# Group 1 joins the block products: its second product with wo3 in seven half-size products, and the sums for wo3 made in group 0's stage 7

## The chip, the core and the metric

One NeuronCore of one Trainium2 chip runs the whole program. The metric is device time in microseconds (us), the median of the runs; lower is better. The engines are TensorE (PE in the profile, its weight loads PEld), VectorE (DVE), ScalarE (ACT), GpSimd (POOL) and SyncE (SP), which issues every DMA of this kernel. Engines take their instructions in order and wait for each other through semaphores.

## The reference

Eight batches of attention through 32 packed rows, then two feed-forward layers over 4608 tokens of width 512, in fp32:

```python
p_packed = sm_attn(p, k, v)              # per head, softmax(p k^T / 8) v
x = sm_attn(q, p_packed, p_packed)       # tokens x 512
x = (silu(x @ w_gate) * (x @ w_val)) @ w_out         # d_ff 1536
a, b = x @ w1, x @ w2                                # d_ff 1024
return (a * b @ w3) @ w_out2                         # w3 1024 x 1024, w_out2 1024 x 512
```

## The kernel before

The change lies in the last layer. `w3 @ w_out2` is multiplied out once, as wo3 (1024 x 512), in pieces between the work of the layer ahead of it; what remains is `(x w1 * x w2) @ wo3`. Every fp32 operand is split into a high and a low part (`split`: a cast on ScalarE, a subtraction on VectorE or GpSimd, line 89 in the profile), and each product is three matmuls: high by high, high by low, low by high.

The tokens go in six groups of 768 (`g`, two halves of TH = 384). A group has two stages.

**Stage 5** (`stage5`, matmuls on line 1111) computes ab = (x w1) * (x w2) for eight blocks `f` of 128 features. Both products over two token halves are done as seven block products (`PROD`: sums and differences of weight blocks, S1 to S4, by sums and differences of x, T1 to T4) instead of eight. The sums accumulate in PSUM banks A, B and C: ScalarE copies bank A after product 0 (`keep("s1", A)`), and product 2 adds to the same bank, so product 2 cannot start before that copy. The weight blocks ws (f, k) are made in group 0 (`ws_sums`, `ws_block`) and stored to DRAM (wsd). From then on they are read back: one by one for group 1 (`ws_load`, line 833), in pairs for groups 2 to 5 (`ws_pair`, line 1018).

**Stage 7** multiplies ab by wo3. Groups 0 and 1 do it plainly (`stage7`, line 1201): per 128 tokens, 8 blocks f by three matmuls of 512 columns, with wo3_hi and wo3_lo held in SBUF. Groups 2 to 5 do it in seven block products (`stage7s`, line 1225): sums of ab (`pair_tasks`) by blocks and sums of wo3, 256 columns wide, whose split halves are loaded from DRAM (wobd, `wob_load`). `GS = 2` is the number of plain groups.

The wobd blocks are made during stage 5 of group 1 (`wob_task`): for each i of four, two rows of wo3 are loaded (wo3e), four differences T1 to T4 formed (line 1051, tile wo3s), seven blocks split (wobs) and stored (line 1059). A table `wob_at` says in which block f and behind which product k each step is issued.

Inputs of the next group, x2, are loaded, subtracted and split by `x2_prep` (lines 838, 843, 89): for the plain groups in four parts just ahead of stage 7.

SBUF is held in pools. `mp` has wo3_hi, wo3_lo and what the plain groups need, `wst` fourteen weight blocks of 256 columns. When the last plain group is done both are released and `mp2` takes their bytes: tile wsx for every fifth pair, kA to kD for the copies out of PSUM, the sums of ab, two blocks wob. All pools are made with `reuse_waits="tile"`: a tile waits for every user of an earlier tile on its bytes. wsx, kC, kB, ab0 and kA, the first tiles of mp2, lie on the bytes of wo3_hi.

This last part stands in `with tc.manual_schedule(...)`: each engine issues in the order in which the program is written. The layer ahead of it (lines 897 to 986) is put in order by a scheduler instead. There, `pin` and `behind` give it hints: while `pin` holds an instruction under a name, an instruction issued through `behind` with that name is kept behind it. `w3_task` converts, transposes and multiplies the rows of w3 and w_out2 in pieces: `w3_conv` converts (through `conv`, whose instructions ask for the pins "act" and "dve"), and `w3_step` transposes and multiplies. `w3_at[1]` and `w3_at[2]` are the last accumulation and the last activation of the first unit of the last batch pair.

Of the kernel before, what the change touches and what calls it, by code (L numbers as in the profile page):

```python
# [8 lines left out]
F32 = mybir.dt.float32  # L9
F32R = mybir.dt.float32r  # L10
# [3 lines left out]
ALU = mybir.AluOpType  # L14
# [24 lines left out]
def packed_attention_moe_kernel(  # L39
# [768 lines left out]
    def ws_tile(g, f, k):  # L808
        if f == 0:
            if k % 2 == 0:  # L810
                wg_at.append(wgv.tile([128, 2, 2, 256], F32R, tag=("wh", "wl")[k // 2 % 2], name=f"ws0_{k}"))
            t = wg_at[-1][:, k % 2]
        else:
            t = wst.tile([128, 2, 256], F32R, tag="wst", name=f"ws{g}_{f}_{k}", bufs=14)
        ws_t[f, k] = t
        return t
# [8 lines left out]
    def ws_at(f, k):  # L825
        i, half = divmod(7 * f + k, 2)
        return wsd[i][:, half]
# [1 line left out]
    def ws_store(f, k):  # L829
        nc.sync.dma_start(ws_at(f, k), ws_t[f, k].bitcast(F32))  # L830

    def ws_load(g, f, k):
        nc.sync.dma_start(ws_tile(g, f, k).bitcast(F32), ws_at(f, k))

    def x2_load(g, i, j):
        t = xp.tile([128, 2, TH], F32, tag="x2r", name=f"x2r{g}_{i}{j}", bufs=3)
        c0 = 2 * TH * g + TH * j
# [40 lines left out]
    def w3_task(P, f, slot):  # L878

        if P < NPR - 1 or slot not in W3S[f % GF] or f > 9 or (f == 0 and slot < 3):  # L880
            return
        i = w3_at[0]
        w3_at[0] += 1
        if 0 < i <= len(w3_list) and w3_list[i - 1].startswith("w3"):
            if NH <= i < 2 * NH:
                pin.update(dve=w3_at[1], act=w3_at[2])
            new = tuple(int(x) for x in w3_list[i - 1].split("_")[1:])
            pin.clear()
            w3_step(new, w3_old[0])
            w3_old[0] = new  # L890
            if new[1] == NF2 - 1:
                w3_step(None, new)
                w3_old[0] = None
        if i < len(w3_list):
            w3_conv(w3_list[i])

    for n, (P, f) in enumerate(steps):
        def at(i):
# [107 lines left out]
    def split_wo3(r):  # L1006
        split(wo3_hi[:, r], wo3_lo[:, r], wo3_t.pop(r))

    GS = 2
    NPB = NF2 // 2  # L1010
    pair_t, wob_t, abT, later = {}, {}, {}, []

# [22 lines left out]

    wo3_b = {}

    def wob_task(i, n):

        if n == 0:  # L1040
            e, o = (vl.tile([128, DM], F32, tag=("vt", "vu")[i % 2], name=f"wo3e{i}_{r}") for r in range(2))
            for r, t in enumerate((e, o)):
                nc.sync.dma_start(t, wo3d[1, 2 * i + r])
            b = wo3_b[i] = {"B11": e[:, 0:256], "B12": e[:, 256:512], "B21": o[:, 0:256], "B22": o[:, 256:512]}
            return
        b = wo3_b[i]
        if n == 1:
            t = xp.tile([128, 4, 256], F32, tag="wf", name=f"wo3s{i}")
            for at, (name, x, y) in enumerate((("T1", "B12", "B11"), ("T2", "B22", "T1"),
                                               ("T3", "B22", "B12"), ("T4", "B21", "T2"))):  # L1050
                nc.vector.tensor_tensor(out=t[:, at], in0=b[x], in1=b[y], op=ALU.subtract)
                b[name] = t[:, at]
            return
        k = n - 2
        if (7 * i + k) % 2 == 0:
            wo3_b["to"] = wgv.tile([128, 2, 2, 256], F32R, tag=("wh", "wl")[(7 * i + k) // 2 % 2], name=f"wobs{i}_{k}")
        t = wo3_b["to"][:, (7 * i + k) % 2]
        split(t[:, 0], t[:, 1], b[PROD[k][2]], sub_on="pool" if k % 2 else "dve")
        nc.sync.dma_start(wobd[k][:, i], t.bitcast(F32))

    wob_at = {}
    for i in range(NPB):
        wob_at[((0, 4), (1, 0), (2, 4), (4, 4))[i]] = [(i, 0)]
        for n in range(1, 7):
            wob_at[2 * i + 1, n] = [(i, n)]
        if i + 1 < NPB:
            wob_at[2 * i + 2, 1], wob_at[2 * i + 2, 2] = [(i, 7)], [(i, 8)]

    def block(i, name, src, on):
        hl = tuple(mp2.tile([128, TH], F32R, tag=f"{name}{x}{i}", name=f"{name}{x}{i}") for x in "hl")  # L1070
# [27 lines left out]
    def stage5(g, f):  # L1098
# [16 lines left out]
        def ahead(k):  # L1115

            if g == 0 and f + 1 < NF2:
                ws_block(f + 1, k)
            n = (NF2 - 1) * g + f + 1
            ng, nf = divmod(n, NF2 - 1)  # L1120
            if f and 0 < ng < GS:
                ws_load(ng, nf + 1, k)
            if g == GS - 1 and f == 0:
                ws_store(0, k)
            i = 56 * (g - GS) + 7 * f + k
            if g >= GS and i % 2:
                pair_t.pop(i // 2)
                ws_pair(i // 2 + 5)
            if g == GS - 1:
                for x in wob_at.pop((f, k), ()):  # L1130
                    wob_task(*x)
            if g >= GS and 0 < k < 6 and later:
                later.pop(0)()

# [56 lines left out]
    def stage7(g):  # L1191
        for tb in range(2 * TH // 128):
            j, cols = tb // 3, slice(128 * (tb % 3), 128 * (tb % 3) + 128)
            t = bank(f"po{g}_{tb}")
            for f in range(NF2):
                abh, abl = ab_t[f]
                for a, w, first, last in (
                    (abh, wo3_hi, f == 0, False), (abh, wo3_lo, False, False),
                    (abl, wo3_hi, False, f == NF2 - 1),
                ):  # L1200
                    nc.tensor.matmul(t, lhsT=a[:, j, cols], rhs=w[:, f], start=first, stop=last)  # L1201
            o = vl.tile([128, DM], F32, tag="vu", name=f"o{g}_{tb}")
            nc.scalar.copy(o, t)
            r0 = 2 * TH * g + 128 * tb
            nc.sync.dma_start(out[r0:r0 + 128, :], o)

    def stage7s(g):
        bkA, bkB = ([bank(f"po{n}{g}_{m}")[:, 0:256] for m in range(3)] for n in "AB")
# [39 lines left out]
    with tc.manual_schedule(engines=M0):  # L1248
        for g in range(NG2):
            for f in range(NF2):  # L1250
                stage5(g, f)
                if g == 0:
                    if f + 2 < NF2:
                        ws_sums(f + 2)
                    if f + 3 < NF2:
                        load_w12(f + 3)
                    split_wo3(f)
                    if f + 1 < NF2:
                        load_wo3(f + 1)
                if g == GS and f in (2, 4, 6):  # L1260
                    wob_load(f // 2 - 1)
            if g < GS:
                ab_split.pop()()
                if g == GS - 1:
                    wob_task(NPB - 1, 7)
                    wob_task(NPB - 1, 8)
                for part in range(4):
                    x2_prep(g + 1, part)
                if g == GS - 1:
                    for n in range(4):  # L1270
                        ws_pair(n)
                stage7(g)
            else:
                if g + 1 < NG2:
                    x2_prep(g + 1, 0)
                while later:
                    later.pop(0)()
                stage7s(g)
            if g == GS - 1:
                assert not wob_at  # L1280
                mp.release()
                wst.release()
                mp2 = pool("mp2", "right")
                ws_pair(4)
# [38 lines left out]
```

## Time and profile before

| | |
|---|---|
| median of 3 runs | 1352.88 us (1351.63 to 1355.17) |
| the profiled execution | 1352.85 us, span 1351.0 us |
| TensorE busy | 1327.5 us, 98% |
| VectorE, ScalarE, GpSimd busy | 734.5, 607.9, 466.1 us |
| group 0, stage 5 and stage 7 | 806.9 to 867.9 to 901.3 us |
| group 1 | 901.3 to 961.2 to 993.9 us |
| group 2 | 993.9 to 1052.4 to 1082.9 us |

The span is the time from the first to the last instruction that the profiler saw; the time of the execution is 1.85 us more. Stage bounds are the starts of the first matmul of each stage. Busy shares are of the span.

### The profile page before, as it was taken

To read this page: it belongs to the slowest core of one execution; us is meant where nothing else is said; L and a number is where in the kernel's file an instruction comes from. 1 tells how busy PE (TensorE), PEld (TensorE's weight loads), DVE (VectorE), ACT (ScalarE), POOL (GpSimd) and SP (SyncE) were. 2 spreads that over 40 slices of the span, in tenths; PEclk is the share of its full clock that TensorE was granted. 3 is DMA by queue.
4 is the path that set the end of the run, shared out by engine and by line. 5 is a ranking of instruction groups with operands and counts; after the bars stand their busy time and mean duration, and the time that the engine had idled before them with its cause. 6 is when DMAs were issued, how large, how long until landed. Compare 5 with 4: busy or idle time off the path is not lost.

```text
span 1351.0 us, 26605 instructions
## 1 busy us (share of the span) xinstructions
PE 1327.5 (98%) x10628; PEld 1251.9 (93%) x10628; DVE 734.5 (54%) x1114; ACT 607.9 (45%) x1068; POOL 466.1 (35%) x385
## 2 busy tenths in 40 slices
PE   8989999999999999999999999999999999999999
PEld 6679899999999999989999999889899999999999
DVE  4766877336564466562363379636535535456352
ACT  5774644244443444344554246435334334345241
POOL 1332322323322333243444226404315245153261
PEclk9999999999999999999999999999999999999999
DMA  9987766524455444234443149949769898978865
GB/s 308 344 241 214 216 194 194 167 74 130 148 128 180 121 127 126 71 124 139 145 148 111 55 164 322 342 138 334 256 234 307 315 308 267 327 252 280 311 205 172
DMA packets 192348, 278.32 MB, mean 206 GB/s; under 512 B 71008, under 2 KB 124256, under 8 KB 189920
## 3 DMA queue, kind: packets, MB, share of 16 engines
q1 hardware_dynamic: 192224, 276.62, 63.6%
q8 instruction: 84, 1.38, 0.4%
q14 instruction: 40, 0.33, 0.1%
HBM read 217.84 MB, written 58.72 MB: 205 GB/s over the span
## 4 chain that ended last, share of the span: by engine, by line
PE 76%; DVE 6%; DMA 4%; issue 1%; ACT 1%; SPq 0%; POOL 0%; DVEq 0%; ACTq 0%; POOLq 0%
PE px L675 19%; PE pA L1111 11%; PE pg L446 10%; PE pv L446 9%; PE pB L1111 6%; PE po L1201 4%; PE poA L1225 4%; PE pw L767 3%; PE poB L1225 3%; PE pC L1111 3%; PE pc L413 2%; DMA x2r<-X2d 1%; DMA wo3r<-wo3d 1%; DVE ws L89 1%; DMA ws<-wsd 1%
## 5 line engine op out<-in xcount | busy, mean ns | idle before, releaser
L89 POOL TENSOR_TENSOR ul<-u,uh 128x576 fp32r<-128x576 f32 x96 | 145.5, 1517 | 304.7 <-ACT uh L96 278.6
L675 PE MATMUL px<-uh,woh 128*128 128x384 f32 x576 | 148.1, 338 | 0.2
L455 DVE TENSOR_TENSOR u<-u,pv 128x576 f32<-128x576 f32 x96 | 72.0, 750 | 139.3 <-PE pv L446 123.5
L675 PE MATMUL px<-ul,woh 128*128 128x384 f32 x576 | 146.6, 335 | 0.0
L675 PE MATMUL px<-uh,wol 128*128 128x384 f32 x576 | 146.5, 335 | 0.0
L96 ACT CAST uh<-u 128x576 fp32r<-128x576 f32 x96 | 64.6, 673 | 111.9 <-DVE u L455 111.7
L687 DVE TENSOR_TENSOR acc<-acc,px 128x768 f32<-128x768 f32 x72 | 67.9, 947 | 79.3 <-PE px L675 78.9
L675 PEld LDWEIGHTS px<-uh,woh 128*128 128x128 f32 x576 | 102.9, 188 | 6.4 <-issue 3.7
L89 POOL TENSOR_TENSOR wol<-wof,woh 128x512 fp32r<-128x512 f32 x48 | 65.2, 1369 | 125.9 <-ACT woh L96 120.9
L675 PEld LDWEIGHTS px<-uh,wol 128*128 128x128 f32 x576 | 104.3, 188 | 0.0
L675 PEld LDWEIGHTS px<-ul,woh 128*128 128x128 f32 x576 | 104.3, 188 | 0.0
L451 ACT ACTIVATE u<-pg 128x576 f32<-128x576 f32 x96 | 62.4, 650 | 87.7 <-PE pg L446 81.4
L446 PE MATMUL pg<-aTh,ch 128*128 128x288 f32 x384 | 84.0, 300 | 1.2 <-DVE cl L89 0.8
L446 PE MATMUL pv<-aTh,ch 128*128 128x288 f32 x384 | 82.9, 297 | 0.9 <-DVE cl L89 0.6
L446 PE MATMUL pg<-aTh,cl 128*128 128x288 f32 x384 | 82.3, 296 | 0.5 <-DVE cl L89 0.5
L446 PE MATMUL pg<-aTl,ch 128*128 128x288 f32 x384 | 82.4, 296 | 0.0
L446 PE MATMUL pv<-aTh,cl 128*128 128x288 f32 x384 | 82.1, 295 | 0.0
L446 PE MATMUL pv<-aTl,ch 128*128 128x288 f32 x384 | 82.0, 295 | 0.0
L446 PEld LDWEIGHTS pg<-aTh,ch 128*128 128x128 f32 x384 | 63.0, 188 | 9.3 <-DVE u L455 3.2
L89 DVE TENSOR_TENSOR cl<-pc,ch 128x1024 fp32r<-128x1024 f32 x48 | 56.8, 1217 | 26.4 <-ACT ch L425 26.4
L446 PEld LDWEIGHTS pv<-aTh,ch 128*128 128x128 f32 x384 | 61.7, 188 | 2.0 <-DVE cl L89 0.8
L446 PEld LDWEIGHTS pg<-aTh,cl 128*128 128x128 f32 x384 | 61.9, 189 | 0.7 <-DVE cl L89 0.7
(415 smaller groups left out, 3443.7 us busy)
## 6 DMA issues: line engine op xcount, KB each, us to landing
wsp<-wsd SPq DMA_DIRECT2D x112, 512.0 KB, 4.4
wf<-Wd SPq DMA_DIRECT2D x36, 512.0 KB, 6.3
wob<-wobd SPq DMA_DIRECT2D x18, 1024.0 KB, 6.2
wsd<-ws SPq DMA_DIRECT2D x56, 256.0 KB, 3.4
ws<-wsd SPq DMA_DIRECT2D x49, 256.0 KB, 5.3
wob<-wobd SPq DMA_DIRECT2D x40, 256.0 KB, 5.2
km<-in_k_dram SPq DMA_DIRECT2D x16, 576.0 KB, 7.6
wof<-wod SPq DMA_DIRECT2D x36, 256.0 KB, 2.9
```

The source lines that it names most:

```text
L89: x = eng.tensor_tensor(out=out, in0=src, in1=hi.bitcast(F32), op=ALU.subtract)
L96: nc.scalar.copy(hi, src)
L413: nc.tensor.matmul(t[hs[at], b, Q], lhsT=PTd[es, 2 * (2 * P + b) + Q, hs[hq]], rhs=w[es, 2 * Q + hq // 2].rearrange("p g n -> p (g n)"), s ...
L446: nc.tensor.matmul(t[:, hf, 0:HS], lhsT=w[:, b % 2, Q, cols], rhs=x[:, Q, hf, :], start=first, stop=last,)
L451: x = nc.scalar.activation(u, t[:, :, 0:HS], AF.Silu)
L455: x = nc.vector.tensor_tensor(out=u, in0=u, in1=t[:, :, 0:HS], op=ALU.mult)
L675: nc.tensor.matmul(t[:, h, 0:CW], lhsT=w[:, 128 * d:128 * d + 128], rhs=x[:, CW * c:CW * c + CW], start=first, stop=last,)
L687: pin_at["acc"] = nc.vector.tensor_tensor(out=o, in0=o, in1=t[:, :, 0:CW], op=ALU.add)
L767: nc.tensor.matmul(t[:, 1], lhsT=a[:, kk], rhs=w, start=(i == 0), stop=(i == 11))
L1111: nc.tensor.matmul(bk[n], lhsT=w[:, hl, 128 * d:128 * d + 128], rhs=r[:, d], start=(first and d == 0 and i == 0), stop=(d == 1 and i == 2) ...
L1201: nc.tensor.matmul(t, lhsT=a[:, j, cols], rhs=w[:, f], start=first, stop=last)
L1225: nc.tensor.matmul(bk[n][m], lhsT=l, rhs=w[i][:, h], start=(first and i == 0 and q == 0), stop=(i == NPB - 1 and q == 2), skip_group_check ...
```

## The change

`GS` becomes 1: group 1 is treated as groups 2 to 5 are. Its weight blocks come in pairs from wsd, and its second product is done in seven block products. `ws_load` goes. The seven weight blocks of f = 0 are stored to wsd at the end of group 0, and the first two rows of wo3 and the first four pairs are loaded there.

The sums for wo3 are made during group 0's stage 7, behind the copy and store of each of its first four output tiles (`wob_make`). Only the four T blocks are formed and split; the plain blocks B11, B22 and B21 are stored straight from wo3_hi and wo3_lo. The split tiles are taken from `wst`. The rows of the next i are loaded (`wob_rows`) behind the subtractions of this one, into the two buffers of "vt".

In `w3_task` the lines that set and clear the pin move from ahead of `w3_step` to around `w3_conv`.

```diff
-    def ws_load(g, f, k):
-        nc.sync.dma_start(ws_tile(g, f, k).bitcast(F32), ws_at(f, k))
...
         if 0 < i <= len(w3_list) and w3_list[i - 1].startswith("w3"):
-            if NH <= i < 2 * NH:
-                pin.update(dve=w3_at[1], act=w3_at[2])
             new = tuple(int(x) for x in w3_list[i - 1].split("_")[1:])
-            pin.clear()
             w3_step(new, w3_old[0])
...
         if i < len(w3_list):
+            if NH <= i < 2 * NH:
+                pin.update(dve=w3_at[1], act=w3_at[2])
             w3_conv(w3_list[i])
+            pin.clear()
...
-    GS = 2
+    GS = 1
...
-    def wob_task(i, n):
...
+    def wob_rows(i):
+        if i < NPB:
+            wo3_b[i] = [vl.tile([128, DM], F32, tag="vt", name=f"wo3e{i}_{r}") for r in range(2)]
+            for r, t in enumerate(wo3_b[i]):
                 nc.sync.dma_start(t, wo3d[1, 2 * i + r])
...
+    def wob_make(i):
+        e, o = wo3_b.pop(i)
+        b = {"B11": e[:, 0:256], "B12": e[:, 256:512], "B21": o[:, 0:256], "B22": o[:, 256:512]}
+        t = xp.tile([128, 4, 256], F32, tag="wf", name=f"wo3s{i}")
+        for at, (name, x, y) in enumerate((("T1", "B12", "B11"), ("T2", "B22", "T1"),
+                                           ("T3", "B22", "B12"), ("T4", "B21", "T2"))):
+            nc.vector.tensor_tensor(out=t[:, at], in0=b[x], in1=b[y], op=ALU.subtract)
+            b[name] = t[:, at]
+        wob_rows(i + 1)
+        for k, (_, _, name) in enumerate(PROD):
+            if name[0] == "T":
+                w = wst.tile([128, 2, 256], F32R, tag="wst", name=f"wobs{i}_{k}", bufs=14)
+                split(w[:, 0], w[:, 1], b[name], sub_on="pool" if k % 2 else "dve")
+                nc.sync.dma_start(wobd[k][:, i], w.bitcast(F32))
+            else:
+                n = 256 * (int(name[2]) - 1)
+                for h, w in enumerate((wo3_hi, wo3_lo)):
+                    nc.sync.dma_start(wobd[k][:, i, h], w[:, 2 * i + int(name[1]) - 1, n:n + 256].bitcast(F32))
...
-            n = (NF2 - 1) * g + f + 1
-            ng, nf = divmod(n, NF2 - 1)
-            if f and 0 < ng < GS:
-                ws_load(ng, nf + 1, k)
-            if g == GS - 1 and f == 0:
-                ws_store(0, k)
...
             nc.sync.dma_start(out[r0:r0 + 128, :], o)
+            if tb < NPB:
+                wob_make(tb)
...
                 ab_split.pop()()
-                if g == GS - 1:
-                    wob_task(NPB - 1, 7)
-                    wob_task(NPB - 1, 8)
                 for part in range(4):
                     x2_prep(g + 1, part)
-                if g == GS - 1:
-                    for n in range(4):
-                        ws_pair(n)
+                for k in range(7):
+                    ws_store(0, k)
+                wob_rows(0)
+                for n in range(4):
+                    ws_pair(n)
                 stage7(g)
```

## Rows read from the trace of the kernel before

**Rows 1.** page, busy us (share of the span) and instructions of each engine

```profile
PE 1327.5 (98%) x10628; PEld 1251.9 (93%) x10628; DVE 734.5 (54%) x1114; ACT 607.9 (45%) x1068; POOL 466.1 (35%) x385
```

**Rows 2.** busy time by stretch, start:end, length, then engines, granted clock, DMA

```profile
867.92:901.35 33.43, 33.17 (x146) 26.89 (x145) 12.03 (x14) 9.64 (x14) 0.91 (x1) 1.00 0.47 168
901.35:961.21 59.86, 59.37 (x337) 57.98 (x336) 35.27 (x57) 28.94 (x66) 25.81 (x25) 1.00 0.89 317
961.21:993.89 32.68, 32.68 (x145) 27.04 (x145) 14.60 (x19) 9.72 (x15) 3.39 (x4) 1.00 0.62 209
993.89:1052.39 58.50, 58.49 (x337) 58.19 (x336) 27.37 (x45) 26.29 (x56) 29.67 (x30) 1.00 0.87 293
1052.39:1082.89 30.50, 30.25 (x254) 30.05 (x253) 16.89 (x27) 11.10 (x23) 2.81 (x3) 1.00 0.89 317
```

**Rows 3.** who waited for whom, TensorE, whole span: total us, times, longest

```profile
PE pc L413 <- DVE acc L687: 3.0, 1, 3.0
```

**Rows 4.** busy time by stretch, around 600 us

```profile
596.70:599.30 2.60, 2.60 (x65) 1.37 (x65) 0.95 (x2) 1.95 (x3) 1.21 (x1) 0.72 0.60 201
599.30:601.30 2.00, 2.00 (x10) 2.00 (x7) 2.00 (x2) 0.54 (x1) 0.20 (x1) 0.51 0.87 189
601.30:604.00 2.70, 2.70 (x17) 2.70 (x17) 1.48 (x4) 1.56 (x2) 0.00 (x0) 1.00 0.96 349
```

**Rows 5.** timeline of ScalarE (start, us, instruction), end of group 0

```profile
871.39 0.62 ACT L96 CAST wo_hi<-wo3r 128x512 fp32r<-128x512 f32 x1 [4.81 <-DMA wo3r<-wo3d]
871.91 0.83 ACT L96 CAST abh<-ab 128x768 fp32r<-128x768 f32 x1
```

**Rows 6.** timeline of VectorE, 587 to 597 us

```profile
587.32 0.71 DVE L750 STREAM_TRANSPOSE w3T(0, 0)_7492<-vt_w 128x512 f32<-128x512 f32 x1
587.95 0.92 DVE L687 TENSOR_TENSOR acc<-acc,px 128x768 f32<-128x768 f32 x1
...
595.10 0.71 DVE L750 STREAM_TRANSPOSE w3T(0, 2)_7656<-vt_w 128x512 f32<-128x512 f32 x1
595.73 0.92 DVE L687 TENSOR_TENSOR acc<-acc,px 128x768 f32<-128x768 f32 x1
```

**Rows 7.** timeline of VectorE, stage 7 of group 0; then sums for wo3

```profile
868.12 0.55 DVE L1181 TENSOR_TENSOR ab<-c,pA 128x384 f32<-128x384 f32 x1 [0.48 <-PE pA L1111]
...
872.78 0.96 DVE L89 TENSOR_TENSOR abl<-ab,abh 128x768 fp32r<-128x768 f32 x1
878.41 0.96 DVE L843 TENSOR_TENSOR x2T<-x2r,x2r 128x768 f32<-128x768 f32 x1 [4.68 <-DMA x2r<-X2d]
...
890.22 0.95 DVE L89 TENSOR_TENSOR xT4l<-x2T,xT4h 128x768 fp32r<-128x768 f32 x1
...
958.38 0.42 DVE L1051 TENSOR_TENSOR wo3s<-wo3e 128x256 f32<-128x256 f32 x1
...
959.51 0.96 DVE L1051 TENSOR_TENSOR wo3s<-wo3e,wo3s 128x256 f32<-128x256 f32 x1
```

**Rows 8.** timeline of SP's DMA issues, end of group 0

```profile
871.38 9.25 SPq L838 DMA_DIRECT2D x2r<-X2d  x4
```

**Rows 9.** instructions on tile wo3e: ns min/median/max; last line us

```profile
L1043 SPq DMA_DIRECT2D wo3e<-wo3d x8: 319/392/643, 905.3 to 943.6; - x8
...
DMA to landing us min/median/max: 3.6/4.8/6.0
```

**Rows 10.** the same for tile wobs

```profile
L89 DVE TENSOR_TENSOR wobs<-wo3s,wobs x12: 496/774/959, 916.7 to 966.0; 128x256 fp32r<-128x256 f32 x12
...
DMA to landing us min/median/max: 2.5/5.1/6.6
```

**Rows 11.** timeline of ScalarE, start of group 2

```profile
994.14 0.59 ACT L1203 COPY o<-po 128x512 f32<-128x512 f32 x1 [3.59 <-PE po L1201]
995.14 0.48 ACT L1147 COPY kC<-pA 128x384 f32<-128x384 f32 x1 [0.41 <-PE pA L1111]
```

**Rows 12.** DMA issues, 900 to 995 us: count, KB each, median us to landing

```profile
wsp<-wsd SPq DMA_DIRECT2D x4, 512.0 KB, 6.1
```

More of the change, by code (lines that the diff above doesn't have):

```diff
@@ L1036, in packed_attention_moe_kernel @@
     wo3_b = {}
-    def wob_task(i, n):
-        if n == 0:
-            e, o = (vl.tile([128, DM], F32, tag=("vt", "vu")[i % 2], name=f"wo3e{i}_{r}") for r in range(2))
-            for r, t in enumerate((e, o)):
+    def wob_rows(i):
+        if i < NPB:
+            wo3_b[i] = [vl.tile([128, DM], F32, tag="vt", name=f"wo3e{i}_{r}") for r in range(2)]
+            for r, t in enumerate(wo3_b[i]):
                 nc.sync.dma_start(t, wo3d[1, 2 * i + r])
[L1044 to L1067, printed above, removed]
+    def wob_make(i):
[16 more added lines that the diff above has]
+                    nc.sync.dma_start(wobd[k][:, i, h], w[:, 2 * i + int(name[1]) - 1, n:n + 256].bitcast(F32))
@@ L1128, in ahead @@
                 ws_pair(i // 2 + 5)
-            if g == GS - 1:
-                for x in wob_at.pop((f, k), ()):
-                    wob_task(*x)
             if g >= GS and 0 < k < 6 and later:
@@ L1263, in packed_attention_moe_kernel @@
                 ab_split.pop()()
-                if g == GS - 1:
-                    wob_task(NPB - 1, 7)
-                    wob_task(NPB - 1, 8)
                 for part in range(4):
                     x2_prep(g + 1, part)
-                if g == GS - 1:
-                    for n in range(4):
-                        ws_pair(n)
+                for k in range(7):
[3 more added lines that the diff above has]
+                    ws_pair(n)
                 stage7(g)
@@ L1279, in packed_attention_moe_kernel @@
             if g == GS - 1:
-                assert not wob_at
                 mp.release()
```

## The prediction

> **What bounds the kernel.** I read the page's busy lines first, then a table of the stages, then who TensorE waits for. TensorE is busy 98% of the span, VectorE, the next busiest, 54% [rows 1]: time goes only where TensorE gets less work or stands idle. The table of stages [rows 2] prices the two kinds of group. Group 1, plain in its second product, takes 59.86 us for stage 5 and 32.68 us for stage 7, together 92.54. Group 2, the first with block products in both, takes 58.50 and 30.50, together 89.00. Past the start, TensorE waits only once for longer than 2 us on another engine, 3.0 us for an accumulation on VectorE [rows 3]. There the granted clock then falls to the lower of its levels, 1.2 GHz: 0.72 over 2.6 us, 0.51 over 2.0 us, 1.00 behind that [rows 4], so 2.6 x 0.28 + 2.0 x 0.49 = 1.7 us are lost on top.
>
> **The change, part by part.** The sum starts from the profiled execution, 1352.85 us (the median of the runs is 1352.88).
>
> *Group 1's products.* Stage 7 has 6 x 8 x 3 = 144 matmuls of 512 columns, the seven block products 7 x 3 x 4 x 3 = 252 of 256. The rows give 227 ns for one and 121 ns for the other, so an eighth fewer columns buy 32.68 - 30.50 = 2.2 us only [rows 2]. The Trainium skill ("TensorE: Matmul & The Clock Gate", the part on 56 against 53.3 ns) has a warm matmul start every N / 2.4 GHz plus 2.5 ns: by it, an estimate, 252 x 109.2 ns = 27.5 us, and the sum would be 3 us lower; the trace does not agree, with 30.5, and the trace decides. Stage 5 of group 1 loses the stalls that the sums for wo3 and 49 reloads of weight blocks put in: 59.86 - 58.50 = 1.4 us [rows 2]. The pair sums that replace its split run on the other engines, as in group 2, within the 58.50.
>
> *End of group 0.* Fourteen of those reloads, issued in the last two blocks f, stood in SP's queue ahead of group 0's stage 7. They held back the last row of wo3, whose cast waited 4.81 us [rows 5], and stage 7 lasts 33.43 us against group 1's 32.68 [rows 2]: 0.75 us comes back. So far 2.2 + 1.4 + 0.75, with the rounding -4.3 us.
>
> *The pin that moves.* In w3_task the pin was set and cleared again before any instruction was issued: it did nothing. Now it stands around w3_conv, for four conversions of w3. From 582 to 596 us VectorE runs just these (vx_w, vt_w, and w3T behind them) in front of the accumulations: the one at 587.95 follows a w3T directly, the one at 595.73 too [rows 6], and this third one is what TensorE's 3.0 us wait is for [rows 3]. Pinned behind the last accumulation of that unit, the conversions go to 605 us or later. I take the whole wait, 2.95 us, and the clock's 1.7: -4.65. The other bound is nothing: a scheduler orders this part, and the conversions may get in the way of something else.
>
> *Where the sums for wo3 go.* All of it moves from the 60 us of a stage 5 into group 0's stage 7, 32.7 us. In order on their engines come: the preparation of group 1's x2; the stores of seven weight blocks, the first two rows of wo3 and four pair loads on SP; then for i = 0 to 3 the copy and store of an output tile, four subtractions, the load of the next two rows, four splits and ten stores. Only one pair of rows fits ("vt" has two buffers), so the rows of i + 1 are asked for after the subtractions of i: a serial chain. Its times on the clock of the trace of before:
> - Start. With the reloads gone the x2 loads land before VectorE is free. That is after the product at 868.12 (0.55), the cast (0.83) and the split (0.96): 870.5. Before, the first x2 subtraction ran at 878.41 and the last split ended at 891.2 [rows 5, 7]; the chain shifts by 7.9 us, to 883.3. If the x2 loads, issued from 871.38 [rows 8], move no earlier, the shift is nil.
> - A round: subtractions 2.1 us (958.38 to 960.47 [rows 7]), issue of a second load 0.4, landing 4.8 [rows 9], together 7.3. The first subtractions end at 885.4, the fourth at 885.4 + 3 x 7.3 = 907.3.
> - The last block stored from wo3_hi is the eighth of the ten stores of i = 3, behind two splits on VectorE (0.8 each [rows 10]) and two issues: 909.7. A store lands in 5.1 us [rows 10]: 914.8.
> - By bytes: from 872.3 on the queue carries 14.4 MB up to that store (7 weight blocks, 8 rows, 15 sums and 4 output tiles of 256 KB, 4 pairs of 512 KB, 23 halves of 128 KB, one x2 block of 384 KB). Group 1 moved 317 GB/s at a DMA share of 0.89 in stage 5, so some 350 at a full one [rows 2]: 41 us, with the last landing 914 or so. I take 914.5.
>
> *Who waits.* The pool mp2 takes over the bytes of mp. A tile there waits for every user of an earlier tile on its bytes, and the first of mp2 (the fifth pair of weights, kC, kB, ab0) lie on wo3_hi, whose users now include 12 stores. ScalarE's first copy of group 1, 0.48 us (the copy at 995.14 in group 2 [rows 11]), writes kC: it ends at 915.0. TensorE comes to group 1 at 867.92 + 32.68 = 900.6, runs two products (2.1 us) and needs this copy at 902.7, since the third product adds to the same bank. Stall: 12.3 us. Behind it the clock is low; the nearest row is the 1.7 us above, and I take that (bounds 0 and twice that, since the wait there was shorter). Queued behind the waiting copy are only later copies; the fifth pair's load waits for the same stores, and has six products, 6.3 us, to land, against a median of 6.1 [rows 12]: nothing more is counted.
>
> *Sum.* 1352.85 - 4.3 - 4.65 + 12.3 + 1.7 = 1357.9 us.
>
> *Bounds.* With the shortest landing, 3.6 us [rows 9], a round is 6.1 and the last store is down at 909.7: stall 7.5, total 1353.1. With the longest, 6.0 and 6.6 for the store, it is down at 919.9: 1363.3. If x2 moves no earlier, 7.9 more: 1365.8.
>
> **Rivals.**
> 1. *The chain keeps pace*, and group 1 starts without a stall: 1352.85 - 4.3 - 4.65 = 1343.9. For it: VectorE, ScalarE and GpSimd are busy 12.0, 9.6 and 0.9 us of the 33.4 of that stage [rows 2]. Against it: a round would have to fall to (902.7 - 0.5 - 5.1 - 2.4 - 885.4) / 3 = 3.1 us, less than the shortest landing. It decides if rows arrive ahead of the subtractions after all.
> 2. *Only ScalarE's order holds the copy*, not the stores, because kC's own bytes are rows stored in the early rounds. The copy then follows the last cast (0.4) and two output copies (1.2): it ends at 907.3 + 2.1 = 909.4, stall 6.7, total 1352.3, no change. For it: kC is small, wo3_hi has eight rows. Against it: waits between pools go by tiles here.
> 3. *The pin brings nothing*: 1362.5. For it: the part is scheduled, not written out. Against it: the instructions that move stand right ahead of the late accumulations [rows 6].
> 4. *The 256-column matmuls keep the pitch per column of the 512-column ones*, 227 / 2 = 113.5 ns, since the short ones wait for data in group 2: 252 x 113.5 = 28.6 us, total 1356.0. The Trainium skill's rule above points the same way. Against it: stage 7 of group 2 is busy for 30.25 of its 30.50 us [rows 2].
>
> **Chances and range.** About 0.3%, here 1348.8 to 1356.9, is what a measurement of this kernel can tell from no change. My forecast, a stall of 9 to 17 us with the pin's gain, has 0.50; a quarter of that lies under 1356.9. Rival 3 has 0.21, nearly all of it slower, rival 2 0.13 and rival 4 0.02, mostly no change, rival 1 0.09, faster; 0.05 is left for a longer stall than the bounds. Slower: 0.37 + 0.18 + 0.05 = 0.60; faster: rival 1 and the low end of rival 2, 0.11; no change: the rest, 0.29. The likeliest case alone is 1354 to 1363; the range that leaves out no more than 2 in 10 is 1349 to 1366.
>
> **What the profile of the changed kernel would show.** Right: group 1 in 58.5 and 30.5 us apart from its first products; no 3 us wait near 593 and no lower clock there; stage 7 of group 0 in 32.7; TensorE waiting in the third product of group 1 for ScalarE's copy, and that copy for a DMA that writes wobd; loads of wo3e some 7 us apart; a granted clock below 1 behind the wait. Wrong: wo3e loads under 5 us apart, x2 subtractions still at 878, the copy held by a cast instead of a store, or a wait near 593 under another name. The largest doubt is the round: each microsecond in it is three in the time.

## The result, and the profile after

The changed kernel takes 1361.09 us (median of 4 runs, 1360.03 to 1361.29) against 1353.09 us (4 runs, 1351.63 to 1355.17) for the kernel before: a ratio of 1.0055, 95% interval 1.0040 to 1.0069. It is slower by about 7.4 us. The profiled execution took 1361.14 us, its span is 1359.0 us.

The page's busy line of the changed kernel, to set beside [rows 1]:

```profile
PE 1323.2 (97%) x10736; PEld 1255.6 (92%) x10736; DVE 738.0 (54%) x1140; ACT 611.4 (45%) x1081; POOL 472.0 (35%) x393
```

TensorE is busy 4.3 us less and the span is 8.0 us longer. Who TensorE waited for in the changed kernel, over the whole span:

```profile
PE pA L1102 <- ACT kC L1129: 12.6, 1, 12.6
PE pk L511 <- DMA km<-in_k_dram: 5.9, 3, 5.3
```

The second line belongs to the start; the kernel before has it too, with 5.4 us. The first is new, and the 3.0 us wait for the accumulation [rows 3] is gone. Busy time by stage of the changed kernel, columns as in [rows 2]: stages 5 and 7 of group 0, then both stages of groups 1 and 2:

```profile
803.20:865.11 61.91, 60.43 (x337) 57.95 (x337) 54.00 (x95) 38.93 (x96) 37.03 (x36) 1.00 0.93 324
865.11:897.79 32.68, 32.68 (x145) 27.03 (x145) 20.87 (x35) 12.59 (x24) 3.48 (x4) 1.00 0.85 300
897.79:970.70 72.91, 60.29 (x338) 59.97 (x337) 30.19 (x54) 28.34 (x62) 30.31 (x30) 0.91 0.90 311
970.70:1001.56 30.86, 30.23 (x253) 30.05 (x253) 16.98 (x27) 11.11 (x23) 3.08 (x4) 1.00 0.95 318
1001.56:1059.80 58.24, 58.24 (x338) 58.24 (x337) 27.14 (x46) 25.54 (x55) 29.58 (x29) 1.00 0.81 278
```

Stage 7 of group 0 now moves 300 GB/s where it moved 168 [rows 2], and its end is no later than TensorE's own work makes it. The price falls at the start of group 1: 72.91 us for a stage 5 that takes 58.24 in group 2. ScalarE's timeline there in the changed kernel (start, us, instruction, in brackets the idle time before it and what ended it):

```profile
897.52 0.58 ACT L1185 COPY o<-po 128x512 f32<-128x512 f32 x1
902.75 0.40 ACT L96 CAST wobs<-wo3s 128x256 fp32r<-128x256 f32 x1 [4.64 <-DVE wo3s L1047]
...
904.33 0.71 ACT L96 CAST wobs<-wo3s 128x256 fp32r<-128x256 f32 x2 [0.55 <-DVE wo3s L1047]
904.94 0.58 ACT L1185 COPY o<-po 128x512 f32<-128x512 f32 x1
908.54 0.59 ACT L1185 COPY o<-po 128x512 f32<-128x512 f32 x1 [3.02 <-DMA out_dram<-o]
912.13 0.48 ACT L1129 COPY kC<-pA 128x384 f32<-128x384 f32 x1 [3.00 <-DMA wobd<-wobs]
```

Three things stand in a row before the copy that TensorE needs: the casts of i = 3, late for want of rows of wo3; an output copy, late because its buffer's last store hasn't landed; and the copy itself, late because of a block store. The profile names a store of a split block (wobs) there, while kC lies on the bytes of wo3_hi; which store ended the wait this view does not tell for certain (the run late_first below moves kC off those bytes). All three are the same queue seen from different places, as the next view says. Busy time by stretch in the changed kernel: first most of stage 7, then from the end of stage 7 over the wait and behind it:

```profile
875.00:897.00 22.00, 22.00 (x99) 18.22 (x98) 12.91 (x24) 7.82 (x17) 2.46 (x3) 1.00 1.00 362
896.90:912.60 15.70, 3.14 (x17) 2.66 (x15) 4.37 (x11) 4.27 (x11) 0.73 (x1) 0.69 1.05 373
912.60:914.50 1.90, 1.84 (x6) 1.84 (x7) 0.00 (x0) 0.39 (x2) 0.00 (x0) 0.50 1.03 326
914.50:916.50 2.00, 2.00 (x8) 2.00 (x7) 0.00 (x0) 0.48 (x1) 0.00 (x0) 0.50 0.89 348
916.50:918.50 2.00, 2.00 (x13) 2.00 (x12) 0.55 (x1) 0.48 (x1) 0.09 (x1) 0.99 0.34 96
```

The DMA engines are full from 875 us on (share 1.00, 362 GB/s), and while TensorE waits (share 1.05, 373 GB/s). Behind the wait the granted clock is 0.50, that is 1.2 of 2.4 GHz, for 3.9 us: 1.95 us more are lost.

The pin works as its line says. VectorE's timeline of the changed kernel, to set beside [rows 6]: the accumulations follow TensorE at once, and the conversions come after 607 us.

```profile
587.50 0.95 DVE L687 TENSOR_TENSOR acc<-acc,px 128x768 f32<-128x768 f32 x1 [2.16 <-PE px L675]
590.62 0.95 DVE L687 TENSOR_TENSOR acc<-acc,px 128x768 f32<-128x768 f32 x1 [2.17 <-PE px L675]
...
608.88 0.70 DVE L750 STREAM_TRANSPOSE w3T(0, 0)_7492<-vt_w 128x512 f32<-128x512 f32 x1
```

### The profile page after: what moved, and what is told of

The parts are those of the page before. It is cut to its first block, busy times and chain, and to the rows that moved or that the text cites. A ratio compares the mean times of both kernels' runs of the same rounds, so it can differ in the third digit from the quotient of the medians.

```text
span 1359.0 us, 26818 instructions
## 1 busy us (share of the span) xinstructions
PE 1323.2 (97%) x10736; PEld 1255.6 (92%) x10736; DVE 738.0 (54%) x1140; ACT 611.4 (45%) x1081; POOL 472.0 (35%) x393
## 4 chain that ended last, share of the span: by engine, by line
PE 81%; DVE 3%; DMA 3%; ACT 1%; issue 1%; SPq 0%; POOL 0%; DVEq 0%; ACTq 0%; POOLq 0%
PE px L675 19%; PE pA L1102 15%; PE pg L446 10%; PE pv L446 10%; PE pB L1102 7%; PE poA L1209 6%; PE poB L1209 4%; PE pC L1102 4%; PE pw L767 3%; PE pc L413 2%; DMA wob<-wobd 1%; PE psq L210 1%; DMA wo3e<-wo3d 1%; DVE x2T L840 1%; DMA wobd<-wobs 1%
## 5 line engine op out<-in xcount | busy, mean ns | idle before, releaser
L1134 POOL TENSOR_TENSOR kC<-kB,kC 128x384 f32<-128x384 f32 x20 | 20.3, 1013 | 127.3 <-ACT kB L1129 127.3
```

The costliest lines, as they stand in the source:

```text
L1134: on.tensor_tensor(out=r, in0=o, in1=t, op=op)
```

## The experiments

The theory after the result: the gain and the pin are as forecast, and the stall at the first copy to kC is the loss. What holds that copy was open between four things: the release of wo3_hi's bytes by the stores, ScalarE's order behind the chain of rows, the order in SP's queue, and the number of bytes that must pass. The runs take these away one by one. All times of the table are set against runs of the kernel before on the same chip; the last column is TensorE's waits over 2 us in or before group 1, apart from the start. These waits, and every view below, are those of one profiled execution, whose own time stands beside them: it is not always near the median (for rows_plain and spread it is the fastest of the runs, for pin_alone and spread_res the slowest).

| run | median us (range, runs) | ratio to before, 95% interval | profiled execution us | waits of TensorE in it |
|---|---|---|---|---|
| changed kernel | 1361.09 (1360.03 to 1361.29, 4) | 1.0055 (1.0040 to 1.0069) | 1361.14 | kC 12.6 |
| pin_alone | 1349.12 (1347.21 to 1353.25, 9) | 0.9969 (0.9957 to 0.9982) | 1353.25 | none (wob 2.1 in group 3) |
| no_pin | 1363.40 (1361.85 to 1364.00, 4) | 1.0072 (1.0054 to 1.0091) | 1363.98 | acc 2.9, kC 13.2 |
| late_first | 1356.30 (1353.38 to 1359.12, 10) | 1.0019 (1.0007 to 1.0031) | 1356.34 | kC 8.7 |
| rows_ahead | 1359.06 (1357.11 to 1360.58, 10) | 1.0033 (1.0022 to 1.0043) | 1360.58 | kC 12.7 |
| plain_early | 1357.75 (1355.26 to 1361.21, 10) | 1.0026 (1.0014 to 1.0037) | 1356.07 | kC 8.5 |
| rows_plain | 1355.37 (1350.90 to 1358.10, 10) | 1.0021 (1.0009 to 1.0034) | 1350.90 | kC 5.9 |
| rows_late | 1356.17 (1354.76 to 1360.55, 10) | 1.0031 (1.0021 to 1.0042) | 1355.99 | kC 9.0 |
| plain_last | 1360.10 (1358.96 to 1360.34, 4) | 1.0057 (1.0042 to 1.0072) | 1358.96 | kC 4.1, wsp 7.3 |
| plain_last1 | 1363.31 (1360.61 to 1363.68, 4) | 1.0077 (1.0058 to 1.0096) | 1363.43 | kC 5.0, wsp 7.6 |
| out_queue | 1357.58 (1356.09 to 1358.35, 7) | 1.0025 (1.0014 to 1.0035) | 1356.16 | wsp 11.0 |
| spread | 1355.58 (1350.78 to 1360.11, 12) | 1.0017 (1.0004 to 1.0029) | 1350.78 | wsp 4.9 in three, the longest 2.4 |
| spread_res | 1352.71 (1347.94 to 1355.40, 12) | 0.9991 (0.9980 to 1.0002) | 1355.40 | wsp 2.9 and 2.3 |

**pin_alone: the kernel before with the moved pin and nothing else.**

```diff
...
         if i < len(w3_list):
+            if NH <= i < 2 * NH:
+                pin.update(dve=w3_at[1], act=w3_at[2])
             w3_conv(w3_list[i])
+            pin.clear()
```

> The kernel before with the moved pin and nothing else. My theory: the four conversions of w3 no longer run in front of the accumulations on VectorE, TensorE's 3.0 us wait near 593 us and the 1.7 us of the low clock behind it go, and nothing else moves: about 1348.4 us, 0.35% faster than before. Rival (the pin brings nothing, and group 0 of the changed kernel starts 3.7 us earlier by chance): 1353.

Measured: (1 - 0.9969) x 1354.0 = 4.2 us faster (2.4 to 5.8). The two stretches of [rows 4], in this run:

```profile
596.70:599.30 2.60, 2.60 (x17) 2.60 (x16) 2.48 (x3) 0.14 (x1) 0.00 (x0) 1.00 0.85 323
599.30:601.30 2.00, 2.00 (x14) 2.00 (x13) 0.30 (x1) 0.00 (x0) 0.00 (x0) 1.00 0.52 206
```

The clock stays up where it fell to 0.72 and 0.51. The term of 4.65 us holds: TensorE comes to group 0's stage 5 at 801.96 us instead of 806.91. The profiled execution, the slowest of the nine, loses this again farther on: group 0's stage 7 takes 35.4 us (862.73 to 898.14) instead of 33.4, and group 3 has the 2.1 us wait for wob.

**no_pin: the changed kernel with the pin put back.** The same lines, taken out of the changed kernel and put where they stood.

> The changed kernel with the pin put back where it was, so that only the second group's block products are left of the change. If the pin's 4.2 us (measured by itself) add to the rest, 1361 + 4 = 1365 to 1366, with the 3.0 us wait of the matmuls on the addition back at 593 us. If the pin only shifts work whose delay the later stall takes up anyway, it is within 1 us of the changed kernel, 1361 to 1362.

The wait on the addition is back with 2.9 us, and the wait at kC is 13.2 us, 0.6 longer. By the ratios the run is 2.3 us above the changed kernel, but the two intervals overlap, so these runs don't tell whether the whole 4.2 us reach the end here. The middle of the two expectations came out; neither is refuted.

**late_first: the late tiles of the following pool are laid over wo3_hi and wo3_lo**, so that kC, ab0 and the fifth pair of weights lie elsewhere. No work changes.

```diff
...
                 mp2 = pool("mp2", "right")
+                for n in (1, 2):
+                    wob_pre[n] = mp2.tile([128, NPB, 2, 256], F32R, tag="wob", name=f"wob{n}", bufs=2)
+                for name in ("A11", "S3", "S1", "S2", "A12", "S4", "A22"):
+                    hl_pre[name] = tuple(mp2.tile([128, TH], F32R, tag=f"{name}{x}3", name=f"{name}{x}3") for x in "hl")
                 ws_pair(4)
```

> The changed kernel, with the tiles of mp2 that are written late (two blocks wob, the sums for i = 3) allocated first, so that they and not kC, kB and the fifth pair lie on the bytes of wo3_hi and wo3_lo. My theory: the copy into kC no longer waits for the stores from wo3_hi; it follows the second last output copy on ScalarE (which ends at 909.1) instead of starting at 912.1, so TensorE's 12.6 us wait falls to about 9.6 and the time to about 1358. Rival (only ScalarE's order holds the copy, the stores do not): no change, 1361.

ScalarE's timeline of this run, at the same place as above:

```profile
906.93 0.58 ACT L1187 COPY o<-po 128x512 f32<-128x512 f32 x1 [2.97 <-DMA out_dram<-o]
907.41 0.48 ACT L1131 COPY kC<-pA 128x384 f32<-128x384 f32 x1
```

The copy to kC now follows the output copy with no wait of its own: the release of wo3_hi's and wo3_lo's bytes was real and worth 3.9 us of the 12.6. The rival, that the stores hold nothing, is refuted. The other 8.7 us are held by what stands before it on ScalarE.

**rows_ahead: all eight rows of wo3 are loaded at once**, into the pool of the weight blocks that has just come free; the chain from round to round is cut.

```diff
-            wo3_b[i] = [vl.tile([128, DM], F32, tag="vt", name=f"wo3e{i}_{r}") for r in range(2)]
+            wo3_b[i] = [wst.tile([128, DM], F32, tag="wst", name=f"wo3e{i}_{r}", bufs=14) for r in range(2)]
...
-        wob_rows(i + 1)
...
-                wob_rows(0)
+                for i in range(NPB):
+                    wob_rows(i)
```

> The changed kernel, with all eight rows of wo3 asked for at once at the end of group 0, into buffers of wst, instead of two at a time behind the subtractions of the two before. The serial chain of my prediction is cut, the bytes ahead of the last store stay the same. If the chain sets the stall: the fourth subtractions end near 896, the last store from wo3_hi lands near 903, the wait falls from 12.6 to about 3 us, time about 1350. If the bytes in the queue set it (the DMA share is 1.05 at 373 GB/s from 897 to 912 in the changed kernel): the last store still lands at 908 or later, wait 8 to 12 us, time 1356 to 1361.

The wait stays, 12.7 us. ScalarE's timeline of this run:

```profile
894.52 0.58 ACT L1184 COPY o<-po 128x512 f32<-128x512 f32 x1 [3.47 <-DMA out_dram<-o]
900.10 0.59 ACT L1184 COPY o<-po 128x512 f32<-128x512 f32 x1 [3.76 <-DMA out_dram<-o]
905.40 0.58 ACT L1184 COPY o<-po 128x512 f32<-128x512 f32 x1 [4.72 <-DMA out_dram<-o]
909.12 0.48 ACT L1128 COPY kC<-pA 128x384 f32<-128x384 f32 x1 [3.13 <-DMA wobd<-wo_lo]
```

No cast waits for a row any more, and the wait is no shorter: in the place of the casts the output copies wait for their own stores, which stand in the queue behind the blocks. The chain of rows, on which the forecast rested, is not what sets the stall. (By the ratios this run is 3 us below the changed kernel, with intervals that just touch; its profiled execution is the slowest of the ten, so what the others saved, if anything, is not known.)

**plain_early: the plain blocks are stored row by row in group 0's stage 5**, as soon as each row is split.

```diff
...
                     split_wo3(f)
...
+                    if f:
+                        plain_store(f - 1)
...
+                plain_store(NF2 - 1)
                 for k in range(7):
                     ws_store(0, k)
```

> The changed kernel, with the plain blocks stored from wo3_hi and wo3_lo during stage 5 of group 0, a row at a time, one block f behind its split, so that group 0's stage 7 carries 3.1 MB less and kC's bytes are free when stage 7 ends. My theory: the wait for the stores goes; what holds the copy into kC is ScalarE's order behind the casts of i = 3, whose rows still come in a chain, each round about 6 us with the lighter queue instead of 7.2: copy at about 902 instead of 912, wait about 3 us, time about 1351, plus up to 1.5 us if stage 5 of group 0, at a DMA share of 0.93, gets slower. Rival (the chain of rows alone sets the stall and the stores nothing): rounds stay 7.2 us, copy at 909, wait 9 to 10 us, time 1358.

The wait at kC is 8.5 us and the time 1357.8, where the theory had 3 us and 1351 and the rival 9 to 10 us and 1358: by the numbers the rival, the chain, came out. But the rounds did not stay at 7.2 us. The rows are asked for at 879.83, 885.85, 893.64 and 899.09 us, 6.4 us apart on average, near the 6 us of the theory; only the first is asked for 14.9 us after the start of stage 7 (864.92) instead of 9.8 us after it, since the last x2 load comes later and the last row's four stores now stand behind it. Stage 5 of group 0 pays too: it was already at a DMA share of 0.93 in the changed kernel, and here it takes 63.7 us (801.25 to 864.92) where it took 61.9, at a share of 0.97. Part of the 3.1 MB was only put elsewhere, and this run does not tell the chain from the bytes.

**rows_plain: the two together.**

> The changed kernel with all eight wo3 rows loaded at the start of group 0's stage 7 and the plain blocks stored in group 0's stage 5. If the row chain is what still held ScalarE once the plain stores were gone (plain blocks early alone: 1357.8 us with a wait of 8.5 us at the first kC), that wait falls under 2 us and the time to about 1350. If the bytes in the one queue are what holds it, the 3.1 MB of plain stores are out of stage 7 but the rows' loads and the output stores still share the queue with the stores of T1 to T4: the wait falls to about 4 to 5 us, 1353 to 1354.

The wait is 5.9 us, in the fastest of ten executions (1350.9 us); the median is 1355.4. By the wait and by the median both expectations were too low, the one from bytes (4 to 5 us, 1353 to 1354) by less. The queue stays full without the chain: the DMA share is 1.03 from 872 to 897 us and 1.07, at 402 GB/s, in the 9 us behind. Against plain_early the wait is 2.6 us shorter, which suggests that with 3.1 MB less in the stage the chain does count for something.

**rows_late: rows_ahead and late_first together**, so that kC waits for no store and no cast for a row.

> The changed kernel with the eight rows loaded at once and the late tiles of the following pool laid over wo3_hi and wo3_lo, so that kC waits for no store and no cast waits for a row. If chain and release wait were the whole stall, the wait at the first kC falls under 2 us and the time from 1356.3 (late tiles alone) to about 1348. If the bytes hold it, the output copies still wait for output stores that are queued behind the block stores, the wait stays at 7 to 9 us and the time at 1355 to 1357.

The wait is 9.0 us, the time 1356.2. The release and the chain together account for no more than the release alone.

**plain_last and plain_last1: the 24 stores of the plain blocks are queued behind stage 7's last output store.** Both have the late tiles over wo3_hi and wo3_lo; the first has the rows at once, as rows_late, the second pair by pair.

```diff
...
             if tb < NPB:
                 wob_make(tb)
+        for k, (_, _, name) in enumerate(PROD):
+            if name[0] == "B":
+                plain_store(k, name)
```

> As the run before it (rows at once, late tiles over wo3_hi and wo3_lo), but the 24 stores of the plain blocks (3.1 MB) are queued behind the last output store of stage 7. If the bytes ahead of the output stores set the stall, stage 7's queue has 3.1 MB (about 8.5 us at 370 GB/s) less ahead of its last copies: the wait at the first kC falls under 2 us, ws_pair(4) and its followers come some microseconds later, and the time is 1346 to 1350. If the chain alone mattered it is no other than the run before it.

> The run before it with the rows loaded pair by pair again. If bytes set the stall, the rows' chain has time enough in the emptier queue: within 1 us of the run before it, 1347 to 1350. If the chain of rows, casts and stores sets a round of its own (7.3 us), four rounds still end about 10 us behind and the time stays at 1355 to 1357.

TensorE's timeline of plain_last, the instructions that waited (start, us, instruction):

```profile
901.22 0.69 PE L1105 MATMUL pA<-xT2h,wsp 128*128 128x384 f32 x1 [4.14 <-ACT kC L1132]
...
917.22 0.69 PE L1105 MATMUL pB<-xT1h,wsp 128*128 128x384 f32 x1 [7.29 <-DMA wsp<-wsd]
```

The expectation of 1346 to 1350 failed, and how it failed tells most: the wait at kC falls to 4.1 us, and a wait of 7.3 us comes up six products later, at the fifth pair of weights, whose load now stands behind the same 3.1 MB. Together 11.4 us, against 9.0 in rows_late, from which only this order differs. Here, whoever is put last in the queue is the one that TensorE waits for. Busy time by stretch in plain_last, from the end of the first wait on (the third line is the second wait):

```profile
901.22:906.40 5.18, 5.18 (x17) 5.18 (x18) 0.55 (x1) 0.81 (x2) 0.00 (x0) 0.54 0.85 288
906.40:909.93 3.53, 3.52 (x21) 3.20 (x19) 1.11 (x2) 0.48 (x1) 2.34 (x3) 1.00 0.82 267
909.93:917.22 7.29, 0.00 (x1) 0.01 (x1) 0.00 (x0) 0.48 (x1) 0.68 (x1) 0.70 0.84 259
917.22:922.90 5.68, 5.68 (x18) 5.68 (x19) 0.56 (x1) 1.78 (x4) 0.48 (x1) 0.50 0.87 332
```

Each wait also brings its own stretch of low clock: 5.18 x 0.46 = 2.4 us and 5.68 x 0.50 = 2.8 us, where one wait of 12.6 us cost 1.95. In two pieces the same stall is dearer.

The DMA engines are not full from 901 to 917 us, at a share of 0.82 to 0.85. SP issues the 24 stores of 128 KB one every 0.5 us, from 901.20 to 912.55 us, and the fifth pair's load only at 913.05: 11.9 us, where 3.1 MB at 370 GB/s would take 8.5. So there the number of transfers sets the pace and not their bytes. In the changed kernel the two limits lie close together: a round has 13 transfers, 6.5 us at this pace, and 2.6 MB, 7.1 us at 370 GB/s. No run takes away one without the other, so how much fewer and larger stores would save stays open.

Loading the rows pair by pair (plain_last1) adds 0.9 us at kC and 0.3 at wsp. Its time, 1363.3 us, is above both of its expectations.

**out_queue: rows_late with stage 7's output stores issued by ScalarE instead of SP.**

```diff
-            nc.sync.dma_start(out[r0:r0 + 128, :], o)
+            nc.scalar.dma_start(out[r0:r0 + 128, :], o)
```

> The changed kernel with the rows loaded at once and the late tiles over wo3_hi and wo3_lo, and with stage 7's output stores issued from ScalarE's own queue instead of SP's, so that they don't stand behind the block stores. If the order in SP's queue is what holds ScalarE's copies, the wait at the first kC falls from 9.0 us to under 2 us and the time from 1356.2 to about 1349. If the bytes that must pass before the next weights are the limit, the same bytes are in front of ws_pair(4) as before: the wait at kC falls, one of about the same length comes up at the wsp tile, and the time stays at 1354 to 1357.

ScalarE's and TensorE's timelines of this run:

```profile
896.19 0.59 ACT L1186 COPY o<-po 128x512 f32<-128x512 f32 x1 [1.77 <-PE po L1184]
897.59 0.48 ACT L1130 COPY kC<-pA 128x384 f32<-128x384 f32 x1 [0.81 <-PE pA L1103]
...
915.65 0.69 PE L1103 MATMUL pB<-xT1h,wsp 128*128 128x384 f32 x1 [11.03 <-DMA wsp<-wsd]
```

ScalarE is now on time: its last output copy waits only for TensorE, and kC is written at 897.6. The wait at kC is gone altogether, and one of 11.0 us stands at wsp. The time is 1357.6 us. Against rows_late the order in the queue decided which instruction TensorE waits for (kC for 9.0 us there, wsp for 11.0 here), and shortened nothing. This run settles it against the order, and for what must pass through the queue before the next weights.

**spread: the bytes taken out of the way.** As out_queue, but wo3_hi and wo3_lo lie in a pool of their own that stays open into group 1's stage 5, and the 24 plain stores are issued there, four after each of the first six f. The tiles that lie on those bytes (wob, the sums for i = 3) follow in a pool mp3, and the first two loads of wob come one f later.

```diff
...
+                if g == GS and f < 6:
+                    for n in range(4 * f, 4 * f + 4):
+                        plain_store((0, 3, 5)[n // 8], n % 8)
+                    if f == 5:
+                        mpw.release()
+                        mp3 = pool("mp3", "left")
```

> The changed kernel with the rows loaded at once, the output stores of stage 7 on ScalarE's queue, and the 24 stores of the plain blocks issued four at a time in group 1's stage 5 behind its weight loads; wo3_hi and wo3_lo lie in a pool of their own until then. If the bytes of stage 7 set the stall, 3.1 MB less in front of the next weights take about 8.5 us out of 12.6, the rest being the output copies' order: no wait over 2 us is left there, and the time is the sum without the stall, 1361 - 12.6 - 1.9 (the clock after it) = 1346 to 1349, at or below the moved pin alone (1349.1). If group 1's stage 5 has no room for 3.1 MB beside its own 310 GB/s, waits of 3 to 6 us in all come up at wsp and wob, and the time is 1350 to 1353.

TensorE's line in the list of waits of this run:

```profile
PE pB L1103 <- DMA wsp<-wsd: 4.9, 3, 2.4
```

No wait is left at kC. 4.9 us in three waits stand at wsp, the largest at 937 to 940 us, among the plain stores. The profiled execution took 1350.8 us, the fastest of twelve; the median, 1355.6, lies above both expectations, with runs up to 1360.1. The mean granted clock was 0.995 and 0.996 in the two longest runs, 0.999 and 1.000 in the two shortest, so the longer ones had more of the low clock; behind which waits, no trace shows.

**spread_res: 1.8 MB less besides.** Group 1's first weight blocks are used where group 0 left them; of the first four pair loads only half of one is left. The rest is as in spread.

```diff
...
+        if n < 4:
+            pair_t[n] = wg_at[n]
+            if n == 3:
+                nc.sync.dma_start(wg_at[3][:, 1].bitcast(F32), ws_at(1, 0))
+            return
```

> The run named spread, but group 1's first weight blocks are used where group 0 left them in SBUF: of the four 512 KB loads of the weight pairs in stage 7 only one half of one (256 KB) is left. If bytes ahead of the next weights are the limit, 1.8 MB less (about 5 us at 370 GB/s) take away the 4.9 us of waits at wsp that the run spread still had: under 1 us of them, and a time of 1346 to 1350, below the moved pin alone or beside it. If the waits at wsp in group 1 come from stage 5's own traffic (its loads, the plain stores and wob), they stay at 3 to 5 us and the time at 1350 to 1355.

The time is 1352.7 us, the kernel before again (ratio 0.9991, 0.9980 to 1.0002), and the waits at wsp stay, 2.9 and 2.3 us, as the expectation from stage 5's own traffic has it. The first of the three waits of spread, 1.3 us near 906 us, is gone. (The waits are those of the slowest of the twelve executions, 1355.4 us.) Busy time by stretch in this run, behind these two waits:

```profile
939.40:941.40 2.00, 2.00 (x6) 2.00 (x7) 0.00 (x0) 0.00 (x0) 0.05 (x1) 0.50 1.06 370
941.40:943.40 2.00, 2.00 (x8) 2.00 (x8) 0.55 (x1) 0.00 (x0) 0.00 (x0) 0.50 1.04 408
943.40:945.40 2.00, 2.00 (x8) 2.00 (x7) 0.00 (x0) 0.48 (x1) 1.16 (x2) 0.50 0.76 268
...
959.60:961.60 2.00, 2.00 (x6) 2.00 (x7) 0.00 (x0) 0.00 (x0) 0.55 (x1) 0.50 1.05 434
961.60:963.60 2.00, 2.00 (x10) 2.00 (x10) 0.55 (x1) 0.30 (x1) 0.00 (x0) 0.76 0.98 406
```

Around both the DMA share is about 1.05: the queue has no room there either. Part of the second wait may be of this version's own making, since SP, from which all loads are issued, stood still just before it. Who SP waited for in this run, from 940 to 960 us, the line that bears on this:

```profile
...
SPq L1034 <- DMA wobd<-wo_hi: 3.1, 1, 3.1
...
```

The tile of the second product's blocks of wo3 lies where wo3_hi was, and its load waits for the last plain stores; the pair loads stand behind it. How much of the 2.3 us this makes was not tried. The two waits take 5.3 us, and the clock behind them 6.0 x 0.50 + 2.0 x 0.50 + 2.0 x 0.24 = 4.5 us: 9.8 us in all, about what the pin and the group's products save (4.65 + 4.3). The fastest version of all is pin_alone; no version that was run with group 1's second product in block products beats it.

## Why the prediction was right, and where it was not

**The whole.** Forecast 1357.9 us, measured 1361.14 in the profiled execution: the direction, the place and the instruction are right, the sum is 3.2 us short. By stage: TensorE reaches group 0's stage 5 at 803.20 instead of 806.91 - 4.65 = 802.26 (0.9; an addition on VectorE at 577.09 before is at 578.14 after, so this much was lost before the pin's place at 582 us; the other versions with the moved pin come there between 801.07 and 803.31); that stage takes 61.91 us instead of the 61.01 of before, 806.91 to 867.92 (0.9; in pin_alone, spread and spread_res it took 60.8 to 61.1); stage 5 of group 1 takes 72.91 instead of 58.50 + 12.3 + 1.7 (0.4); its stage 7 takes 30.86 instead of 30.50 (0.4); the later groups 0.3, and the time around the span 0.3. No single term is far off in size.

**The products of group 1.** Right: 30.86 us for the seven block products against 32.68. Rival 4, with 28.6 us, is refuted: the next group needs 30.03 for them.

**The end of group 0.** Right: stage 7 takes 32.68 us, no more than group 1's did, although VectorE and ScalarE do more in it.

**The pin.** Right: 4.65 forecast, 4.2 us measured alone. Rival 3 is refuted.

**The stall.** Forecast 12.3 us and 1.7 for the clock, measured 12.6 and 1.95, at the third product, behind ScalarE's first copy, and that copy behind a DMA to wobd. The step that failed is the one before: "a round", the serial chain of loading rows, subtracting and loading the next, 7.3 us long, three of them behind the first. The loads do stand 7 to 9 us apart (issued from 874.88, 882.00, 891.03 and 897.89 us), but with the chain cut (rows_ahead) the wait is the same 12.7 us. The rounds are that long because each puts 2.6 MB into one queue that moves 360 to 373 GB/s: 2.6 MB / 370 = 7.1 us; 7.2 are measured from one round's first subtraction to the next. The line "By bytes" of the prediction, 14.4 MB and 41 us, kept there as a second way to the same number, was the cause itself, with the number of transfers close behind it (plain_last). That a chain of latencies and a count of bytes come to the same 7 us is luck: the forecast of the stall rested on the wrong one and was right in size. So the statement that each microsecond in the round is three in the time falls too.

**Who waits.** Half right. The release of wo3_hi's bytes is real (late_first: 3.9 us), but it is the last of several waits in a row. Rival 2, ScalarE's order alone, gave 6.7 us and 1352.3; with the release taken away the wait was 8.7 us and the time 1356.3, for the copies stood behind their output stores. And "nothing more is counted" for the fifth pair of weights holds only as long as kC is later: in out_queue that load is the one that TensorE waits 11.0 us for.

**Rival 1**, the chain keeps pace, asked whether rows arrive ahead of the subtractions. In rows_ahead they do, and the stall stays: the condition was put on the wrong resource. What would have to hold is that 14.4 MB pass in the 32 us of the stage, 450 GB/s, more than any stretch shown here.

The Trainium skill ("DMA: Bandwidth & Descriptors", section "Queues, rings and completion order") says that SP's and ScalarE's queues each have a ring on the same 16 DMA engines, and that an engine takes turns between the rings. The runs agree as far as they go: on ScalarE's queue the output stores no longer hold up its copies (out_queue), and the sum of what moves is not more, 360 GB/s at a share of 1.05 from 896 to 904.6 us. The turns themselves no run here shows.

## What to carry to other kernels

When work is moved into another stage, add up the bytes that this stage must then move and set them against its length, before any chain of latencies: here 14.4 MB at 370 GB/s take 39 us, in a stage of 33 us whose queue can only start 5 us in. With the same bytes ahead of the fifth pair of weights, another layout, prefetching, another order and a second queue left 8.7 to 12.7 us of waits somewhere; taking the plain stores out of the stage brought them to between 4.9 and 8.5. Count the transfers too, where they are small: 24 stores of 128 KB took 11.9 us to issue. Test a one-line edit that stands beside a large one by itself: the pin was the whole of what these runs gained.

## What the runs showed of the hardware that was not expected

- The cost of the low clock behind a wait doesn't follow the wait's length. Behind waits of 12.6, 7.3, 4.1, 2.9 and 2.3 us it took 1.95, 2.8, 2.4, 3.0 and 1.5 us. In plain_last and spread_res two shorter waits brought more low clock than the one long one of the changed kernel.
- SP issued 24 stores of 128 KB one every 0.5 us, and the DMA engines were then busy for a share of 0.82 to 0.85 only, at 259 to 288 GB/s (plain_last).
- The 16 DMA engines moved 373 GB/s over 15.7 us and 434 in one stretch of 2 us, loads and stores mixed, above the 350 that the prediction had worked out from a share of 0.89.
